# One staging buffer in place of two, and ten bias tiles in place of nine, in a fused attention and MLP kernel

## The chip, the cores and the metric
The kernel runs on one core of a Trainium2 chip. The time is that of one execution in device microseconds; a kernel is run several times and the median stands for it.

## The reference, cut to what matters
Attention with a position bias made by a small MLP, and then two MLPs, the output of each feeding the next, all in float32:

```
scores = (q @ k.T) / sqrt(64) + bias[h]          # 4 batches x 8 heads, 576 x 576
attn   = exp(scores - max) / sum                 # over the last axis
x      = (attn @ v) as 2304 tokens x 512
h = x @ w_in ;  x = (h * cos(h)) @ w_out         # 512 -> 2048 -> 512
h = x @ w_in2;  out = (max(h,0) + alpha*min(h,0)) @ w_out2
bias[h, i, j] = relu(log1p|i-j| / log1p(max(i,1)) * w1 + b1) @ w2
```

Weights are stored as float64. The kernel turns each into float32 on the chip and splits it into a high part (float32r) and a low part (the rest); a product is then three matrix products, high by high, high by low and low by high.

## The kernel before, in words
Tile, the framework, keeps a program order (the order in which the Python code makes the instructions), puts the instructions of each engine into an order of its own when all are known, and adds the waits. Engines and DMA queues execute in the order that it chose. A pool of tiles has a fixed number of buffers; a tile that finds none free waits for the last use of an older one.

The stages follow one another: the bias of all heads is written to DRAM (`bias_phase`); attention over 16 pairs (4 head pairs by 4 batches, the batch running fastest); `h_phase0` (first product of the first MLP, PE with one unit of 24 matmuls after another in three PSUM units); `o_phase(0)`; `h_phase1`; `o_phase(1)`. Attention runs 9 score blocks a pair; for each, PE makes the scores S (line 480), DVE adds the bias tile `bt` and takes the minimum (line 496), ACT takes the exponential (line 509); then PE transposes, ACT and DVE copy, and PE multiplies by v (lines 596 and 599). From pair 2's second unit on, lists fix the order of PE's work.

A pair of heads has nine bias tiles, one for each block, loaded on SP's queue by `load_bias` (line 417); they serve the four batches of a head pair. In the last batch, the loads of the next head pair's tiles are made block by block, each behind the last use of a tile. `BTB` (line 40) is the number of buffers: nine.

Beside attention, weights for `h_phase0` and `o_phase(0)` are prepared by generators that `step` advances a few pieces at a time, in program order:
- `wi` (line 302) does one of the 16 blocks of w_in: ACT, DVE and POOL turn it into float32 (`conv`), POOL makes the high part (line 316) and the low part (line 320). The first six stay in SBUF; the other ten go into a staging tile `st`, and an SP DMA writes them to `w_d` (line 323). `h_phase0` loads them again.
- `stage_wo` (line 273) does two blocks of w_out at a time: two `conv`, four sums of halves on DVE into the tile `ct` (line 280), then four groups in `leave_w` (line 259). For k from 3 to 7, five jobs, each group goes into a staging tile `sw`: ACT writes the high part (line 253), POOL the low part (line 255), and SP writes the tile to `w2_d` with one DMA (first group) or two (the other three), line 270. I call such a group a leaf.

`st` and `sw` share the tag `st`. During attention the tag lives in the pool `wst` with two buffers, which is closed at the end of attention (`sstack`). The pool `wt` has one buffer of the tag, used from `h_phase0` on, and one of `ct`.

Of the kernel before, what the change touches and what calls it, by code (L numbers as in the profile page):

```python
# [10 lines left out]
F32R = mybir.dt.float32r  # L11
# [25 lines left out]
HP, LP, XP, CPRI, SP = 200, 0, 300, -50, 400  # L37
HIA, LOP = 2, 1
UPB, EPB = {"D": 11, "A": 4}, 6
PBUF, BTB = 6, 9  # L40
FIRST, SIDE, SMOD, BFIRST, BRATE, SPL, WS0, WSR, PER = 4, 6, 2, 8, 2.5, 3, 28, 3.2, 1.0
SR = 2.0
NSP = 2
# [30 lines left out]
def attn_mlp_kernel(ctx: ExitStack, tc: tile.TileContext, a: dict, out: bass.AP):  # L74
# [95 lines left out]
    wpool = {}  # L170
# [7 lines left out]
    cstack = ExitStack()  # L178
    rstack = ExitStack()
    astack = ExitStack()  # L180
    sstack = ExitStack()
    raws_w = {}
    pinned = []
    anchor = []
# [32 lines left out]
    def conv(layer, f, part, box):  # L217
        nm = f"{layer}_{f}_{part}"
        if (layer, f, part) not in raws_w:
            load_raw(layer, f, part)  # L220
            yield
        raw = raws_w.pop((layer, f, part))
        signed = layer == 1 and part == 1
        if wide:
            c = wpool["c"].tile([128, 512], I32, tag="c", name=f"wc{nm}")
            p = wpool["c"].tile([128, 512], I32, tag="p", bufs=1, name=f"wp{nm}")
            hold(se.activation(out=c.bitcast(F32), in_=raw[:, :, 1].bitcast(F32), func=AF.Copy, scale=2.0 ** -112))
            hold(se.activation(out=p, in_=raw[:, :, 0].bitcast(U32), func=AF.Copy, scale=2.0 ** -29))
            yield
            if signed:  # L230
                ve.tensor_scalar(c, c, 3, zs[:, f:f + 1].bitcast(I32), op0=ALU.logical_shift_left, op1=ALU.bitwise_xor)
            else:
                hold(ve.tensor_scalar(c, c, 3, None, op0=ALU.logical_shift_left))
            hold(ve.scalar_tensor_tensor(out=c, in0=raw[:, :, 1], scalar=-2 ** 31, in1=c,  # L234
                                         op0=ALU.bitwise_and, op1=ALU.bitwise_xor))
            yield
            ge.tensor_tensor(out=c, in0=c, in1=p, op=ALU.add)  # L237
            yield
            box.append(c.bitcast(F32))
        else:  # L240
            if signed:
                ve.tensor_scalar(raw, raw, sgn[:, f:f + 1], None, op0=ALU.mult)
                yield
            box.append(raw)
# [7 lines left out]
    def split_to(hi, lo, w, eng=None):  # L252
        hold(se.activation(out=hi, in_=w, func=AF.Copy))
        yield
        hold((eng or (ve if pinned else ge)).tensor_tensor(out=lo, in0=w, in1=hi.bitcast(F32), op=ALU.subtract))
        yield
# [3 lines left out]
    def leave_w(layer, k, g, x):  # L260
        ps = GRPS[layer][g]
        n = len(ps)
        if (layer == 0 and k < NIP) or (layer == 1 and g < 3):
            w = WO[layer, g]
            yield from split_to(w[:, :, k, 0, :], w[:, :, k, 1, :], x)
            return
        st = wpool["t" if pinned else "st"].tile([128, 2, 2, 256], F32R, tag="st", name=f"sw{layer}_{k}_{g}")
        yield from split_to(st[:, 0:n, 0, :], st[:, 0:n, 1, :], x)
        for i, p in enumerate(ps):
            (ge if pinned else sy).dma_start(out=w2_d[layer][SLOT[p], :, k], in_=st[:, i].bitcast(F32))  # L270
        yield
# [3 lines left out]
    def stage_wo(layer, k):  # L275
        box = []
        yield from conv(layer, 2 * k, 1, box)
        yield from conv(layer, 2 * k + 1, 1, box)
        ct = wpool["t"].tile([128, 4, 256], F32, tag="ct", name=f"wt{layer}_{k}")
        sub = lambda o, u, v, op=ALU.subtract: hold(ve.tensor_tensor(out=o, in0=u, in1=v, op=op))  # L280
        c0, c1, c2, c3 = (ct[:, i] for i in range(4))
        u1, u2 = halves_of(box[0])
        v1, v2 = halves_of(box[1])
        if layer == 0:
            sub(c0, u2, v2, ALU.add)
            sub(c3, u1, u2)
            yield
            sub(c1, c0, u1)
            sub(c2, v1, c1)
            yield  # L290
            order = (cols(u1, 1), ct[:, 0:2], ct[:, 2:4], cols(box[1], 2))
        else:
            sub(c0, u2, u1)
            sub(c2, v2, u2)
            yield
            sub(c1, v2, c0)
            sub(c3, v1, c1)
            yield
            order = (cols(u1, 1), ct[:, 0:2], cols(box[1], 2), ct[:, 2:4])
        for g, x in enumerate(order):  # L300
            yield from leave_w(layer, k, g, x)

    def wi(layer, f):
        box = []
        yield from conv(layer, f, 0, box)
        if layer:
            t = wt[f] = wpool["h"][(f + 1) % 4].tile([128, 2, 512], F32R, tag="w", name=f"v{f}")
        elif f < NDIR:
            t = wt[f] = wpool["a"].tile([128, 2, 512], F32R, tag="w", name=f"w{f}")
        else:  # L310
            t = wpool["st"].tile([128, 2, 2, 256], F32R, tag="st", name=f"st{f}").rearrange("p a b c -> p a (b c)")
        hi, lo = t[:, 0], t[:, 1]
        if layer:
            se.activation(out=hi, in_=box[0], func=AF.Copy)
        elif HIA == 2:
            keep(0, ge.tensor_copy(out=hi, in_=box[0]))
        else:
            keep(0, se.activation(out=hi, in_=box[0], func=AF.Copy))
        yield
        keep(1, (ve if layer else ge).tensor_tensor(out=lo, in0=box[0], in1=hi.bitcast(F32), op=ALU.subtract))  # L320
        yield
        if not layer and f >= NDIR:
            sy.dma_start(out=w_d[f], in_=t.bitcast(F32))
            yield

    JOBS = [(wi, (0, f), 1.0, [(0, f, 0)]) for f in range(NF)]
    JOBS += [(stage_wo, (0, k), 3.0, [(0, 2 * k, 1), (0, 2 * k + 1, 1)]) for k in range(NIP, NK)]
    bg = []
# [24 lines left out]
    def attention():  # L353
        with ExitStack() as c:
# [63 lines left out]
            def load_bias(hp, s):  # L418
                t = bt_p.tile([128, S], F32, tag="bt", name=f"bt{hp}_{s}")
                if s == 0:  # L420
                    for i in range(2):
                        sy.dma_start(out=t[64 * i:64 * i + 64], in_=bias_rows(2 * hp + i, 512, S))
                else:
                    h, i = divmod(s - 1, 4)
                    rows = bias_rows(2 * hp + h, 128 * i, 128 * i + 128)
                    if h:
                        sy.dma_start(out=t[:, 64:S], in_=rows[:, 0:512])
                        sy.dma_start(out=t[:, 0:64], in_=rows[:, 512:S])
                    else:
                        sy.dma_start(out=t, in_=rows)  # L430
                bt[hp, s] = t
# [233 lines left out]
            def more_bias(g):  # L665
                nonlocal ng
                while ng < min(g, NG):
                    next(bias)
                    ng += 1
                    if ng >= SIDE and ng % SMOD == 0:  # L670
                        next(side, None)
                    for s, m in GNEED.items():
                        if ng == m:
                            for h in range(2 if s else 1):
                                load_bias(0, s + 4 * h)
                    if ng == NG:
                        for _ in side:
                            pass
                        bstack.close()
                        right = dict(side="right", reuse_waits="tile")  # L680
                        wpool["s"] = rstack.enter_context(tc.tile_pool(name="ws", bufs=2, **right))
                        wpool["c"] = rstack.enter_context(tc.tile_pool(name="wc", bufs=2, **right))
                        wpool["t"] = astack.enter_context(tc.tile_pool(name="wt", bufs=1, **right))
                        wpool["a"] = astack.enter_context(tc.tile_pool(name="wa", bufs=NDIR, **right))
                        wpool["x"] = astack.enter_context(tc.tile_pool(name="xh0", bufs=NCC, **right))
                        wpool["st"] = sstack.enter_context(tc.tile_pool(name="wst", bufs=2, **right))

            pend_exp = []
            fill = []
# [8 lines left out]
            while i < NS or pend_exp or waiting or fill:  # L698
                new = []
                if i < NS:  # L700
# [3 lines left out]
                    hp, b = pairs[n]  # L704
                    more_bias(max(BFIRST + int(BRATE * j), GNEED[s]))
                    for m in range(FIRST, NP):
                        f = pos[m, 1]
# [38 lines left out]
                else:  # L746
                    while fill and credit > 0:
                        d, fn, _ = fill.pop(0)
# [339 lines left out]
    def h_phase1():  # L1088
        runs = [[(0, 512), (512, 1024)], [(1024, 1536), (1536, 2048)], [(2048, 2304)]]
        with ExitStack() as c:  # L1090
# [38 lines left out]
            for k in range(NK):  # L1129
                for _ in range(2):  # L1130
                    if nw < NF:
                        bg.append(wi(1, nw))
                        nw += 1
                bg.append(stage_wo(1, k))
# [39 lines left out]
            step(1000)  # L1174

    attention()
    sstack.close()
    pinned.append(1)
    h_phase0()
    astack.close()  # L1180
# [70 lines left out]
```

## Time and profile before
| what | us |
|---|---|
| median of 3 runs | 1095.66 (1094.87 to 1096.27) |
| the profiled execution's own time | 1095.88 |
| its span in the trace | 1094.1 |
| PE busy | 1054.6 (96%) |
| DVE busy | 801.8 (73%) |
| ACT busy | 642.1 (59%) |
| POOL busy | 229.6 (21%) |

Shares are of the whole span. The slices of the page show PE at 8 tenths in those of 246 to 322 us, and at 9 tenths from there to the end. A stage is read best by its own stretch: the `wi` blocks are done until about 251 us, the five `stage_wo` jobs of attention between 248 and 328 us, attention's last product ends at 337 us.

### The profile page before, as it was taken

To read this page: it belongs to the slowest core of one execution; us is meant where nothing else is said; L and a number is where in the kernel's file an instruction comes from. 1 tells how busy PE (TensorE), PEld (TensorE's weight loads), DVE (VectorE), ACT (ScalarE), POOL (GpSimd) and SP (SyncE) were. 2 spreads that over 40 slices of the span, in tenths; PEclk is the share of its full clock that TensorE was granted. 3 is DMA by queue.
4 is the path that set the end of the run, shared out by engine and by line. 5 is a ranking of instruction groups with operands and counts; after the bars stand their busy time and mean duration, and the time that the engine had idled before them with its cause. 6 is when DMAs were issued, how large, how long until landed. Compare 5 with 4: busy or idle time off the path is not lost.

```text
span 1094.1 us, 18708 instructions
## 1 busy us (share of the span) xinstructions
PE 1054.6 (96%) x7024; PEld 891.2 (81%) x7024; DVE 801.8 (73%) x1292; ACT 642.1 (59%) x1076; POOL 229.6 (21%) x236
## 2 busy tenths in 40 slices
PE   6899999999889999999999999999999999999998
PEld 1346677777667889888899999988888889999998
DVE  7876778788875878778788777677756847777673
ACT  7995788788884555555454554466555534444442
POOL 0005676675550000010000000323222300000000
PEclk9899999999999999999999999999999999999999
DMA  9765748577659433436569171877655649554621
GB/s 331 213 174 159 229 140 293 199 237 253 220 182 390 163 136 128 146 135 229 205 208 306 46 254 66 334 253 224 221 202 185 222 165 358 161 201 130 217 72 46
DMA packets 107594, 219.76 MB, mean 201 GB/s; under 512 B 11504, under 2 KB 57328, under 8 KB 106096
## 3 DMA queue, kind: packets, MB, share of 16 engines
q1 hardware_dynamic: 77104, 157.74, 44.6%
q10 hardware_dynamic: 27968, 50.34, 12.2%
q0 software_dynamic: 2432, 10.49, 2.5%
q8 instruction: 55, 0.90, 0.3%
q14 instruction: 35, 0.29, 0.1%
HBM read 133.98 MB, written 84.56 MB: 200 GB/s over the span
## 4 chain that ended last, share of the span: by engine, by line
PE 78%; DVE 7%; DMA 6%; ACT 4%; issue 2%; POOL 1%; SPq 0%; ACTq 0%; DVEq 0%; POOLq 0%
PE v L1145 18%; PE h L811 16%; PE ob L1014 14%; PE oc L1014 9%; PE oa L1014 8%; PE S L480 5%; DVE P L496 2%; PE x_B L599 2%; PE T_A L574 1%; PE bps L142 1%; DVE wc L234 1%; ACT be L156 1%; PE T_B L574 1%; DMA w_d<-sw 1%; PE x_A L599 1%
## 5 line engine op out<-in xcount | busy, mean ns | idle before, releaser
L1145 PE MATMUL v<-x,v 128*128 128x512 f32 (+1 forms) x984 | 198.0, 364 | 0.0
L1145 PEld LDWEIGHTS v<-x,v 128*128 128x128 f32 x984 | 168.5, 189 | 29.5
L811 PE MATMUL h<-xhi,w 128*128 128x512 f32 (+1 forms) x640 | 183.9, 372 | 1.2 <-DMA w<-w_d 1.2
L237 POOL TENSOR_TENSOR wc<-wc,wp 128x512 int32<-128x512 int32 x64 | 86.5, 1351 | 285.6 <-DVE wc L234 232.7
L811 PEld LDWEIGHTS h<-xhi,w 128*128 128x128 f32 x640 | 116.0, 188 | 23.4 <-DVE tb L825 1.6
L996 ACT ACTIVATE op<-a 128x768 fp32r<-128x768 f32 x84 | 70.5, 844 | 84.6 <-PE ob L1014 27.3
L811 PE MATMUL h<-xlo,w 128*128 128x512 f32 (+1 forms) x320 | 118.7, 371 | 0.0
L997 DVE TENSOR_TENSOR op<-a,op 128x768 fp32r<-128x768 f32 x84 | 80.0, 956 | 51.7 <-ACT op L996 49.4
L496 DVE CUSTOM_DVE_ANT_0 P<-S,bt 128x576 f32<-128x576 f32 x128 | 91.8, 750 | 25.7 <-PE S L480 18.1
L509 ACT ACTIVATE P<-P,nm 128x576 f32<-128x576 f32 x128 | 99.1, 777 | 15.9 <-DVE nm L496 15.8
L996 ACT ACTIVATE op<-b 128x768 fp32r<-128x768 f32 x84 | 70.6, 844 | 62.5 <-PE ob L1014 22.2
L997 DVE TENSOR_TENSOR op<-b,op 128x768 fp32r<-128x768 f32 x84 | 79.7, 954 | 28.0 <-ACT op L996 27.7
L820 ACT ACTIVATE ta<-h,quart 128x1024 int32<-128x1024 f32 x36 | 40.1, 1114 | 67.7 <-PE h L811 48.5
L1156 DVE SCALAR_TENSOR_TENSOR u<-v,asg,u 128x1024 f32<-128x1024 f32 (+2 forms) x48 | 48.0, 1013 | 40.8 <-ACT u L1155 40.4
L1014 PE MATMUL ob<-op,wo 128*128 128x384 f32 x432 | 76.4, 336 | 0.0
L1014 PEld LDWEIGHTS ob<-op,wo 128*128 128x128 f32 x432 | 75.1, 188 | 0.0
L821 DVE SCALAR_TENSOR_TENSOR tb<-ta,h 128x1024 f32<-128x1024 int32 x36 | 43.8, 1218 | 35.1 <-ACT ta L820 33.5
L811 PEld LDWEIGHTS h<-xlo,w 128*128 128x128 f32 x320 | 60.4, 189 | 11.1
L1155 ACT ACTIVATE u<-v,sgn 128x1024 f32<-128x1024 f32 (+2 forms) x48 | 42.9, 897 | 41.7 <-PE v L1145 41.6
L234 DVE SCALAR_TENSOR_TENSOR wc<-raw,wc 128x512 int32<-128x512 int32 x64 | 59.8, 938 | 1.2
L824 ACT ACTIVATE tb<-tb,hpi 128x1024 f32<-128x1024 f32 x36 | 41.2, 1144 | 22.7 <-DVE tb L822 21.0
L1014 PE MATMUL oc<-wq,op 128*128 128x256 f32 x432 | 53.3, 283 | 0.2 <-DVE op L997 0.2
(154 smaller groups left out, 2077.9 us busy)
## 6 DMA issues: line engine op xcount, KB each, us to landing
a<-g_d SPq DMA_DIRECT2D x60, 384.0 KB, 4.5
g_d<-tb ACTq DMA_DIRECT2D x36, 512.0 KB, 2.9
b<-g_d SPq DMA_DIRECT2D x48, 384.0 KB, 4.9
raw<-in_wi_dram SPq DMA_DIRECT2D x32, 512.0 KB, 3.8
raw<-in_wo_dram SPq DMA_DIRECT2D x32, 512.0 KB, 4.2
g_d<-u ACTq DMA_DIRECT2D x28, 512.0 KB, 2.8
bias_d<-be SPq DMA_DIRECT2D x36, 295.5 KB, 3.4
w_d<-sw SPq DMA_DIRECT2D x35, 256.0 KB, 2.8
```

The source lines that it names most:

```text
L234: hold(ve.scalar_tensor_tensor(out=c, in0=raw[:, :, 1], scalar=-2 ** 31, in1=c, op0=ALU.bitwise_and, op1=ALU.bitwise_xor))
L237: ge.tensor_tensor(out=c, in0=c, in1=p, op=ALU.add)
L480: pe(te.matmul(ps[:, hf, 0:HS], lhsT=w[r, 128 * i:128 * i + 128], rhs=m[r, c0:c0 + HS], start=(j == 0), stop=(j == len(terms) - 1)))
L496: keep(2, ve.tensor_tensor_reduce(out=sn.rearrange("p (a b) -> p a b", a=2), in0=ps[:, :, 0:HS], in1=bt[hp, s].rearrange("p (a b) -> p a b ...
L509: exps.append(se.activation(out=e, in_=e, func=AF.Exp, bias=nm, scale=-1.0, accum_out=sums[n, u][:, col, 0:1]))
L811: te.matmul(ps[:, i], lhsT=w_[:, wx, w], rhs=xx[:, 0:n], start=(j == 0), stop=(j == 11))
L821: ve.scalar_tensor_tensor(out=g, in0=tt, scalar=-C1, in1=h, op0=ALU.mult, op1=ALU.add)
L996: se.activation(out=o[:, 0], in_=x, func=AF.Copy)
L997: lows.append(ve.tensor_tensor(out=o[:, 1], in0=x, in1=o[:, 0].bitcast(F32), op=ALU.subtract))
L1014: ins = te.matmul(ps[:, m], lhsT=x[:, sl] if L else w[:, sl], rhs=w if L else x, start=first, stop=kk == NK - 1 and n == 2, skip_group_che ...
L1145: ins = te.matmul(both[:, i, 0:a1 - a0], lhsT=w[:, wx, 128 * cc:128 * cc + 128], rhs=x[:, xx, cc, a0 - o:a1 - o], start=(n == 0), stop=(n ...
L1156: ve.scalar_tensor_tensor(out=g, in0=ps, scalar=asg[:, f:f + 1], in1=g, op0=ALU.mult, op1=ALU.max)
```

## The change
Ten bias tiles in place of nine. The pool `wst` with its two buffers goes; the staging tiles of attention, of `wi` and of `stage_wo`, are taken from the one buffer of the tag in the pool `wt`, which stays open to the end of `h_phase0`. Per partition that is 8192 bytes less and 2304 bytes more; tiles that lie behind the bias tiles move by 2304 bytes. What is computed is the same. The float32 scores of the first four pairs and the fixed lists from pair 2's second unit on, which the change's name also speaks of, are in both kernels.

```
-PBUF, BTB = 6, 9
+PBUF, BTB = 6, 10
...
-    sstack = ExitStack()
...
-        st = wpool["t" if pinned else "st"].tile([128, 2, 2, 256], F32R, tag="st", name=f"sw{layer}_{k}_{g}")
+        st = wpool["t"].tile([128, 2, 2, 256], F32R, tag="st", name=f"sw{layer}_{k}_{g}")
...
-            t = wpool["st"].tile([128, 2, 2, 256], F32R, tag="st", name=f"st{f}").rearrange("p a b c -> p a (b c)")
+            t = wpool["t"].tile([128, 2, 2, 256], F32R, tag="st", name=f"st{f}").rearrange("p a b c -> p a (b c)")
...
-                        wpool["st"] = sstack.enter_context(tc.tile_pool(name="wst", bufs=2, **right))
...
     attention()
-    sstack.close()
```

## Rows read from the trace of the kernel before

**Rows 1.** Windows: busy us and (instructions) of each engine, clock, DMA share, GB/s.
```profile
166.00:246.00 80.00, 77.25 (x705) 59.72 (x704) 64.02 (x158) 64.78 (x150) 56.73 (x58) 1.00 0.73 241
246.00:322.00 76.00, 65.58 (x588) 49.81 (x586) 64.20 (x151) 64.06 (x144) 42.09 (x40) 1.00 0.64 217
322.00:337.00 15.00, 14.79 (x101) 10.69 (x100) 4.51 (x11) 6.82 (x14) 3.02 (x3) 1.00 0.93 311
337.00:350.00 13.00, 11.79 (x52) 9.46 (x51) 9.37 (x10) 7.53 (x8) 1.28 (x1) 1.00 1.03 402
```
**Rows 2.** Timeline of DVE: the last instruction of a pair (start, duration).
```profile
148.95 0.49 DVE L615 TENSOR_TENSOR xe_B<-x_B,T_B 128x320 f32<-128x320 f32 x1
...
245.96 0.49 DVE L615 TENSOR_TENSOR xe_B<-x_B,T_B 128x320 f32<-128x320 f32 x1
...
282.58 0.49 DVE L615 TENSOR_TENSOR xe_B<-x_B,T_B 128x320 f32<-128x320 f32 x1
...
302.09 0.48 DVE L615 TENSOR_TENSOR xe_B<-x_B,T_B 128x320 f32<-128x320 f32 x1
...
321.93 0.47 DVE L615 TENSOR_TENSOR xe_B<-x_B,T_B 128x320 f32<-128x320 f32 x1
```
**Rows 3.** Chain of waits around attention's end (start, us, what).
```profile
339.06 10.06 DMA w<-w_d
349.26 111.79 PE h L811 x576
```
**Rows 4.** Timeline: leaves of three jobs on ACT, POOL and SP.
```profile
259.85 0.63 ACT L253 ACTIVATE sw<-wt 128x512 fp32r<-128x512 f32 x1 [0.27 <-DVE wt L280]
...
288.62 0.62 ACT L253 ACTIVATE sw<-wt 128x512 fp32r<-128x512 f32 x1
289.68 2.70 POOL L255 TENSOR_TENSOR sw<-wt,sw 128x512 fp32r<-128x512 f32 x2
289.69 0.61 ACT L253 ACTIVATE sw<-wt 128x512 fp32r<-128x512 f32 x1
290.97 0.80 SPq L270 DMA_DIRECT2D w_d<-sw  x2
...
299.16 0.42 ACT L253 ACTIVATE sw<-wc 128x256 fp32r<-128x256 f32 x1 [0.63 <-DMA w_d<-sw]
...
319.75 0.61 ACT L253 ACTIVATE sw<-wt 128x512 fp32r<-128x512 f32 x1
```
**Rows 5.** DMA issues: KB each, median us to landing; of 284 to 303 us.
```profile
w_d<-sw SPq DMA_DIRECT2D x8, 256.0 KB, 2.6
```
**Rows 6.** The same of 320 to 360 us, and of the whole span.
```profile
w_d<-sw SPq DMA_DIRECT2D x6, 256.0 KB, 5.7
...
w_d<-st SPq DMA_DIRECT2D x10, 512.0 KB, 4.6
```
**Rows 7.** ACT's instructions of `conv`, 262 to 322 us, by line.
```profile
L228 ACT ACTIVATE wp<-raw 128x512 int32<-128x512 uint32 x7 | 4.7, 673 | 4.1 <-POOL wc L237 4.1
L227 ACT ACTIVATE wc<-raw 128x512 f32<-128x512 f32 x7 | 4.7, 668 | 0.0
```
**Rows 8.** Waits of ACT, 245 to 330 us: total, times, longest.
```profile
ACT sw L253 <- DMA w_d<-sw: 2.1, 3, 0.9
```
**Rows 9.** Tile `sw`, 245 to 290 us: spread of the landings.
```profile
DMA to landing us min/median/max: 2.1/2.6/4.7
```
**Rows 10.** Waits of DVE, 262 to 322 us.
```profile
DVE wt L280 <- POOL wc L237: 2.5, 4, 1.1
```
**Rows 11.** Timeline of POOL and SP: two `wi` blocks.
```profile
212.32 1.28 POOL L320 TENSOR_TENSOR st<-wc,st 128x512 fp32r<-128x512 f32 x1
213.54 0.61 POOL L316 CAST st<-wc 128x512 fp32r<-128x512 f32 x1
214.60 0.38 SPq L323 DMA_DIRECT2D w_d<-st  x1
```
**Rows 12.** Waits of SP, 165 to 246 us, and of POOL, 240 to 262 us.
```profile
SPq L430 <- DVE nm L496: 3.6, 6, 0.8
...
POOL qh L458 <- DMA rq<-in_q_dram: 4.1, 1, 4.1
```
**Rows 13.** Waits of 322 to 360 us at PE.
```profile
PEld h L811 <- DVE tb L825: 1.6, 1, 1.6
PE h L811 <- DMA w<-w_d: 1.2, 1, 1.2
```

## The prediction
> **What bounds the kernel now.** I read the engines' busy time by stretch first, then the chain of waits, then the stretch that the change touches instruction by instruction. From 349 us on the chain of waits is PE, one matmul behind the other [rows 3]; nothing that the change does after attention lasts long enough to alter that. So the time is set by when PE gets through attention and through the change to the first MLP.
>
> Attention has two regimes. Beside the blocks of w_in, PE is busy 77.25 of 80 us [rows 1], and a pair takes (245.96 - 148.95)/6 = 16.17 us [rows 2]: PE is the bound. Beside the w_out jobs it is busy 65.58 of 76 us [rows 1], and a pair takes (321.93 - 245.96)/4 = 18.99 us [rows 2]. ACT and DVE are busy 64 of these 76 us each, about 84%, and in order; PE waits for them. PE idles 10.4 us there against 2.6 in as much time of the first regime: 7.8 us is the most that any relief can bring back. From 322 to 337 us PE is busy again (14.79 of 15), since units of the first MLP fill in, while ACT is busy for 6.8 and DVE for 4.5 us [rows 1]: there is room for displaced work.
>
> **The change part by part.** *A slower chain of leaves.* Now, with two buffers, a leaf's ACT instruction follows the one before it after 1.07 us (288.62, 289.69) [rows 4]. With one it waits until the DMAs of that leaf have landed: ACT at 288.62, POOL's low part until 291.0 (half of the 2.70), two DMA issues until 291.8, the second begun at 291.4, landing 2.6 us later [rows 5], so at 294.0. That is 5.4 us a leaf; the first leaf of a job, half as large with one DMA, I estimate at 4.4. A job thus takes at least 3 x 5.4 + 4.4 = 20.6 us, where the trace has (319.75 - 259.85)/4 = 14.98 [rows 4]. The last job's second leaf moves from 319.75 to about 259.85 + 4 x 20.6 = 342 us, behind attention.
>
> *Relief.* In 76 us there are 76/20.6 = 3.7 jobs in place of 5.1. A job is 2 x (0.668 + 0.673) + 3 x 0.62 + 0.42 = 4.96 us of ACT [rows 4, 7], so about 6.9 us of ACT leave the crowded stretch (and its share of DVE's and POOL's work) for the roomy one behind it. That lies between nothing and the 7.8 us above; since the load of a pair falls only by some 10%, I take half: -3.9.
>
> *New waits on ACT.* Behind a leaf's instruction on ACT stand the exponentials and the copies out of PSUM; DVE and PE wait for these. The order of ACT is fixed ahead, so a leaf costs what the landing is later than that order allows for. The trace shows this only where a third leaf came too soon for two buffers: three waits of 2.1 us in all, 0.7 each [rows 8]. Bounds: 0, where the order allows for the whole landing (other work then goes ahead), and 4.7 - 2.6 = 2.1 us, the longest landing over the median [rows 9]. Some 12 leaves fall into the crowded stretch: 12 x 0.7 = 8.4 us of waiting (0 to 25). ACT has 11.9 us idle there [rows 1], in which part of it disappears: the pair with the 0.63 us wait [rows 4] took 302.09 - 282.58 = 19.51 us and the next, without one, 19.84 [rows 2], so a wait isn't simply added. I take half, the value between none and all: +4.2 (0 to +12.6).
>
> The Trainium skill, in PSUM — Partial Sum Buffer, Engine vs sequencer instructions, says that the queues of ScalarE, VectorE and GpSimdE are strictly first in, first out. By that alone every microsecond of a leaf's wait would be paid by all behind it, 8.4 in place of 4.2 us; these two pairs don't bear it out as a price, since the engine had idle time anyway.
>
> *Tiles held longer.* `ct` and the converted blocks are read by the late leaves, so the next job's sums on DVE and conversions on ACT wait. Nearest are DVE's waits for the job's own data, 2.5 us in four [rows 10]: 0.6 for each of four jobs, half hidden as above: +1.2 (0 to +2.5).
>
> *The blocks of w_in.* Here POOL waits. The low part of a block ends at 213.60, its DMA is issued at 214.60 [rows 11] and lands 4.6 us later [rows 6], at 219.2; the next block's high part, now at 213.54, starts 5.7 us later. POOL has 23.3 us idle in 80 [rows 1], the next pair of blocks comes a pair later, and PE isn't waiting for POOL: 0. If that cover goes, a late split of q and k holds up S; I allow up to +2.
>
> *The tenth bias tile.* Nine tiles are in use until the last batch, so a load waits for the tile of its own block; six such waits on SP took 3.6 us over two head pairs' change [rows 12]. The tenth lets each load use the tile freed a block earlier. What is late next are the loads of q behind them in SP's queue, for which POOL waited 4.1 us once [rows 12], and a bias tile is needed only a pair later. At most -1; I take 0. The shift by 2304 bytes changes which attention tiles the first MLP's weights wait for; 0, within the bounds below.
>
> *The change to the first MLP.* Three leaves of the last job now fall at about 342, 347 and 353 us, where the DMA engines are full (share 1.03) [rows 1] and such a transfer lands after 5.7 us, 3.1 more [rows 6]. Each can hold ACT for that long in front of the first MLP's activations. PE waited there once already, 1.6 us for DVE [rows 13], so the three PSUM units cover only part of 3 x 3.1: I take +2 (0 to +5). The weights on which PE waited 1.2 us [rows 13] can come sooner, as fewer writes precede them, or later, if a load of w_out that needs the last job's first leaf stands in front of them in SP's queue: 0 (-1.2 to +3).
>
> Sum: -3.9 + 4.2 + 1.2 + 0 + 0 + 2 + 0 = +3.5 us on the profiled execution's own 1095.88, 1099.4. That execution is 0.2 above the median, so 1099.2 us.
>
> **The rivals.** *Relief wins.* The order allows for the landings, ACT hardly waits, and the work goes where there is room. For it: only 2.1 us of such waits in 20 leaves now [rows 8]. Against it: in all but a few of them the second buffer was there. -3.9 to -7.8, with +1 to +2 at the change of stage: about -4.5, 1091.
>
> *ACT and DVE pay every wait.* At 84% the engines have little slack of the right kind; each leaf's wait is passed on whole: -3.9 + 8.4 + 2.5 + 2 = +9, 1104.7. It decides from about 0.7 us a leaf on. Against it: the two pairs named above. The Trainium skill's rule of the strict queues would make it this one.
>
> *Nothing moves.* Most leaves' waits fall into idle time, and the relief is as small: ±1, 1095.7. For it: idle 11.9 us of ACT [rows 1]. It is also what would be seen if the tenth tile and the one buffer were both off the path.
>
> **How the numbers follow.** A measurement here can't tell less than 0.2%, 2.2 us, from no change. The forecast's case has 0.50, between about -1 and +7: 0.34 slower, 0.13 within, 0.03 faster. Relief 0.22: 0.19 faster, 0.03 within. Every wait paid 0.13, slower. Nothing moves 0.15: 0.13 within, 0.01 on each side. Together faster 0.23, same 0.29, slower 0.48. The range takes in the middle of the relief and all but the worst of the paid waits: 1090 to 1107; the likeliest case alone has 1095 to 1103.
>
> **What would show it.** Leaves some 5.4 us apart on ACT and jobs 20 us apart; the last leaves behind 340 us; ACT's waits for the DMAs of `sw` at 8 us or so in place of 2.1. Pairs of 18 to 20 us between 246 and 322 us: at 17 the relief has won, at 21 every wait is paid. PE's wait for the first MLP's weights near 1.2 us, and waits of ACT for `sw` behind 340 us with some idle time of PE behind them. Pairs at 16.2 us before 246 us, or the step on w_in's blocks is wrong. If the leaves are not much farther apart than now, the first step is wrong and all behind it.

## The result and the profile after

| kernel | median, us (runs) | ratio to before, 95% interval |
|---|---|---|
| before | 1095.41 (6) | 1 |
| after | 1104.74 (6) | 1.0083 [1.007, 1.0096] |

The change made the kernel 0.83% slower. The profiled execution of after is its slowest one, 1108.48 us, with a span of 1106.7 us; before's span was 1094.1.

Four stretches as in [rows 1], and one behind them (columns as there):
```profile
166.00:246.00 80.00, 75.28 (x680) 58.26 (x680) 61.63 (x150) 63.16 (x145) 52.25 (x53) 1.00 0.70 226
246.00:322.00 76.00, 66.81 (x556) 51.42 (x552) 50.82 (x129) 55.01 (x124) 29.95 (x31) 0.93 0.48 156
322.00:337.00 15.00, 14.51 (x116) 10.62 (x113) 9.71 (x26) 10.48 (x24) 5.42 (x6) 1.00 0.58 180
337.00:350.00 13.00, 11.83 (x73) 8.67 (x72) 4.63 (x8) 4.78 (x8) 3.29 (x3) 1.00 0.95 335
...
350.00:420.00 70.00, 66.54 (x286) 53.21 (x285) 56.12 (x61) 39.67 (x50) 15.53 (x13) 1.00 0.70 258
```
DVE and ACT are much less busy beside the leaves (50.82 and 55.01 us, 64 each before): work has left this stretch, though it also holds a little less of the pairs. But PE's mean clock falls to 0.93: 66.81 x 0.07 = 4.7 us of full speed lost. Beside w_in, PE is idle for 4.72 us instead of 2.75, and between 350 and 420 us for 3.46 instead of nothing (70.00 of 70.00 busy before).

Pair ends, as in [rows 2], and attention's last:
```profile
150.87 0.49 DVE L614 TENSOR_TENSOR xe_B<-x_B,T_B 128x320 f32<-128x320 f32 x1
...
249.80 0.49 DVE L614 TENSOR_TENSOR xe_B<-x_B,T_B 128x320 f32<-128x320 f32 x1
...
285.97 0.49 DVE L614 TENSOR_TENSOR xe_B<-x_B,T_B 128x320 f32<-128x320 f32 x1 [0.85 <-PE x_B L595]
308.50 0.48 DVE L614 TENSOR_TENSOR xe_B<-x_B,T_B 128x320 f32<-128x320 f32 x1
329.38 0.48 DVE L614 TENSOR_TENSOR xe_B<-x_B,T_B 128x320 f32<-128x320 f32 x1
346.52 0.49 DVE L614 TENSOR_TENSOR xe_B<-x_B,T_B 128x320 f32<-128x320 f32 x1 [3.79 <-PE x_B L595]
```
The pair between the third and the fourth of these took 22.5 us, where before's took 19.5. Attention ends 9.4 us later (337.16 before); what follows takes 760.2 us instead of 756.9.

Leaves on ACT, as in [rows 4] (the bracket is the idle time before the instruction and what ended it):
```profile
273.79 0.41 ACT L252 ACTIVATE sw<-wc 128x256 fp32r<-128x256 f32 x1
280.63 0.63 ACT L252 ACTIVATE sw<-wt 128x512 fp32r<-128x512 f32 x1 [1.97 <-DMA w_d<-sw]
286.97 0.62 ACT L252 ACTIVATE sw<-wt 128x512 fp32r<-128x512 f32 x1
293.80 0.63 ACT L252 ACTIVATE sw<-wc 128x512 fp32r<-128x512 f32 x1 [3.53 <-DMA w_d<-sw]
300.71 0.41 ACT L252 ACTIVATE sw<-wc 128x256 fp32r<-128x256 f32 x1
...
398.06 0.63 ACT L252 ACTIVATE sw<-wt 128x512 fp32r<-128x512 f32 x1 [1.31 <-DVE wt L279]
```
Here they stand 6.3 to 6.9 us apart and a job takes 26.9 (273.79 to 300.71; the next one takes 24.3). Eight of the twenty start behind attention, the last of them at 412.75 us, 66 behind. PE at the fourth of them:
```profile
294.96 1.22 PE L595 MATMUL x_A<-T_A,v 128*128 128x256 f32 x2 [2.85 <-ACT T_A L558]
```
The copy T_A stands right behind the leaf in ACT's order (294.33), so the leaf's wait of 3.53 us became 2.85 us of idle PE. The windows behind it:
```profile
293.00:296.00 3.00, 1.04 (x3) 0.86 (x4) 0.00 (x0) 2.21 (x5) 1.27 (x1) 0.72 0.02 7
296.00:299.00 3.00, 3.00 (x15) 2.98 (x14) 1.19 (x3) 1.97 (x5) 0.00 (x0) 0.50 0.60 219
299.00:302.00 3.00, 3.00 (x22) 2.38 (x22) 2.03 (x4) 1.77 (x5) 0.74 (x1) 0.64 0.00 0
```
The granted clock is 0.50, the lower of its two levels (1.2 GHz), right after that idle time. It happens again between 317 and 323 us (0.71 and 0.72 in two windows of 3 us).

Waits of 245 to 330 us (as [rows 8]), and waits at PE of 340 to 420 us (as [rows 13]):
```profile
ACT sw L252 <- DMA w_d<-sw: 8.4, 4, 3.5
...
PE h L809 <- DVE tb L823: 2.7, 2, 2.3
```
PE's wait for the first MLP's weights is 0.7 us, 1.2 before. The last block of w_in is now written at 269.96 us, 18.6 later than before (251.34):
```profile
269.96 0.32 SPq L322 DMA_DIRECT2D w_d<-st  x1
```

### The profile page after: what moved, and what is told of

Read it like the earlier page. It is cut to its first block, busy times and chain, and to the rows that moved or that the text cites. A ratio compares the mean times of both kernels' runs of the same rounds, so it can differ in the third digit from the quotient of the medians.

```text
span 1106.7 us, 18702 instructions
## 1 busy us (share of the span) xinstructions
PE 1058.9 (96%) x7024; PEld 894.9 (81%) x7024; DVE 800.7 (72%) x1292; ACT 644.0 (58%) x1076; POOL 230.1 (21%) x236
## 4 chain that ended last, share of the span: by engine, by line
PE 72%; DVE 9%; DMA 8%; ACT 5%; issue 3%; POOL 1%; SPq 1%; ACTq 0%; POOLq 0%; DVEq 0%
PE v L1143 18%; PE ob L1012 14%; PE oc L1012 9%; PE oa L1012 8%; PE h L809 8%; PE S L479 5%; DMA w_d<-sw 3%; PE x_B L598 2%; PE T_B L573 2%; DMA w<-w_d 2%; PE bps L142 2%; DVE P L495 2%; PE T_A L573 1%; DVE tb L819 1%; DVE wc L233 1%
## 5 line engine op out<-in xcount | busy, mean ns | idle before, releaser
L233 DVE SCALAR_TENSOR_TENSOR wc<-raw,wc 128x512 int32<-128x512 int32 x64 | 54.8, 859 | 1.4
L1012 PE MATMUL ob<-wp,op 128*128 128x256 f32 x432 | 52.8, 282 | 0.0
```

The source lines that it names most:

```text
L1012: ins = te.matmul(ps[:, m], lhsT=x[:, sl] if L else w[:, sl], rhs=w if L else x, start=first, stop=kk == NK - 1 and n == 2, skip_group_che ...
```

## The experiments

By ratio to before, times 1095.4 us:

| kernel | tiles, leaf's high part on | ratio, interval | us against before |
|---|---|---|---|
| e1 one buffer | nine, ACT | 0.9985 [0.9974, 0.9996] | -1.6 |
| after | ten, ACT | 1.0083 [1.007, 1.0096] | +9.1 |
| e8 one buffer | nine, POOL | 0.9939 [0.9925, 0.9954] | -6.7 |
| e4 one buffer | ten, POOL | 0.9962 [0.9948, 0.9976] | -4.2 |
| e6 one buffer | ten, order of nine, ACT | 0.9993 [0.9984, 1.0003] | -0.8 |
| e10 one buffer, later jobs | nine, ACT | 1.0072 [1.005, 1.0095] | +7.9 |
| e9 one buffer, later jobs | ten, ACT | 1.0057 [1.0037, 1.0077] | +6.2 |

**One staging buffer alone.** The kernel after with nine tiles:
```
-PBUF, BTB = 6, 10
+PBUF, BTB = 6, 9
```


> One staging buffer, nine bias tiles. Theory A (the single staging buffer costs the time; the tenth tile is off the path): 1104 us, within 2 of the changed kernel's 1104.7. Rival B (the tenth tile and the shift of the tiles behind it cost it): 1096 to 1098. Rival C (the tenth tile gains a little that the staging buffer's loss covers): 1107 or more.

Measured: 1094.89 us, 0.9985, so theory A falls. The staging buffer costs nothing here, though the leaves are late as well and ACT waits for their landings 16.3 us in eleven instructions (245 to 420 us; 2.1 before). Its stretches from 246 us on, three pair ends, and the first leaves of two jobs:
```profile
246.00:322.00 76.00, 68.70 (x615) 52.27 (x614) 58.96 (x146) 60.23 (x137) 34.46 (x35) 1.00 0.53 182
322.00:337.00 15.00, 14.15 (x83) 10.54 (x82) 7.15 (x15) 8.10 (x17) 5.44 (x6) 1.00 0.79 272
337.00:350.00 13.00, 11.54 (x51) 9.18 (x51) 9.29 (x8) 7.36 (x8) 3.20 (x2) 1.00 1.03 401
350.00:420.00 70.00, 68.79 (x298) 55.44 (x297) 60.56 (x68) 39.69 (x51) 14.95 (x11) 1.00 0.64 230
```
```profile
245.91 0.49 DVE L614 TENSOR_TENSOR xe_B<-x_B,T_B 128x320 f32<-128x320 f32 x1
...
316.86 0.47 DVE L614 TENSOR_TENSOR xe_B<-x_B,T_B 128x320 f32<-128x320 f32 x1
336.30 0.48 DVE L614 TENSOR_TENSOR xe_B<-x_B,T_B 128x320 f32<-128x320 f32 x1
```
```profile
310.51 0.42 ACT L252 ACTIVATE sw<-wc 128x256 fp32r<-128x256 f32 x1
...
332.46 0.42 ACT L252 ACTIVATE sw<-wc 128x256 fp32r<-128x256 f32 x1 [1.43 <-DMA w_d<-sw]
```
The clock stays at 1.00. Four pairs take 70.95 us where before's took 75.97 [rows 2]: 5.0 us gained. The last pair takes 19.4 us where before's took 15.2, but 2.1 of these 4.2 us are matmuls of the first MLP done earlier (8.87 us of them in that pair, 6.81 before). PE's idle time says it more directly: against before it is 3.1 us less from 246 to 322 us, and from 322 to 420 us it is 2.1 more (3.52 against 1.42). The Trainium skill, in Trainium Kernel Development and Optimization, Best Practices, advises double-buffering for performance; here, at this pace of the jobs, one buffer in place of two was, if anything, 0.15% faster.

**One buffer for one of the two stages.** Both kernels keep before's two buffers; a dummy tile holds one, either from the first block of w_in to the first leaf (e2, cut here to where the tile is taken) or from there to the last leaf (e3):
```
...
+            wpool["hold"] = wpool["st"].tile([128, 2, 2, 256], F32R, tag="st", name="taken")
+            ge.memset(wpool["hold"].bitcast(F32)[:, 0, 0, 0:1], 0.0)
...
```


> Nine bias tiles, two staging buffers, one of which a dummy tile holds until the first leaf of w_out: one buffer for the blocks of w_in, two for the leaves. If the loss comes from the leaves (theory A1): 1096 to 1098, and the blocks of w_in end at about 270 us in place of 251 with pairs still near 16.5 us. If it comes from POOL's waits and the late start of the leaves (theory A2): 1100 to 1105. Both halves: about 1100, as the late start pushes leaves behind attention.

> Nine bias tiles, two staging buffers for the blocks of w_in, and one for the leaves of w_out, the other held by a dummy tile from the first leaf to the last. Theory A1 (the leaves cost it): 1101 to 1104, ACT's waits for the DMAs of the leaves 8 us or more inside attention. Theory A2 (the blocks of w_in cost it): 1096 to 1097.

Measured: 1118.8 us, 1.0205 [1.0188, 1.0221], and 1124.38, 1.0252 [1.0231, 1.0273]. Both are far slower than after and outside every range that I had named. Waits of e2, 330 to 420 us:
```profile
PE h L815 <- DVE tb L829: 20.5, 1, 20.5
...
ACT sw L253 <- DMA w_d<-sw: 13.6, 2, 11.3
```
PE stands still for 20 us at the change to the first MLP (27.7 in e3), and the clock falls to 0.80 to 0.85 over 350 to 420 us. In this layout, with the pool of two buffers open to attention's end, late leaves meet the start of the first MLP; in e1, with late leaves too but one buffer, PE has no such stop. The stop hides what the runs were to tell apart, so they don't say which of the two stages pays.

**The leaf's high part on POOL.** In `split_to`, for the leaves of attention:
```
...
-        hold(se.activation(out=hi, in_=w, func=AF.Copy))
+        if on_pool:
+            hold(ge.tensor_copy(out=hi, in_=w))
+        else:
+            hold(se.activation(out=hi, in_=w, func=AF.Copy))
...
-        yield from split_to(st[:, 0:n, 0, :], st[:, 0:n, 1, :], x)
+        yield from split_to(st[:, 0:n, 0, :], st[:, 0:n, 1, :], x, on_pool=not pinned)
```
e4 is the kernel after with this, e8 is e1 with it, e7 is the kernel before with it, and e2p is e2 with it.

> The changed kernel, with the high part of a leaf written by POOL instead of ACT during attention: the chain of leaves is as long or longer (1.3 us in place of 0.6 on the first step at most), but ACT no longer waits for a landing. If ACT's waits in order are the price (theory A1): 1097 to 1100, pairs of 16.5 to 18 us between 250 and 330 us. If the late leaves behind attention or PE's lower clock of their own are the price: 1103 to 1107.

> One staging buffer, nine bias tiles, and the high part of a leaf on POOL instead of ACT. ACT waited 16 us for leaves in the same kernel with ACT. If such waits are paid even where the sum came out even (theory P: relief hides them): 1087 to 1091, better than the kernel before. If they fell into idle time: 1093 to 1095.

> The kernel before (two buffers, nine tiles), with the high part of a leaf on POOL. ACT waits only 2.1 us for leaves there, and 2.3 us of ACT's work a job move to POOL. Theory P: 1090 to 1094, a gain by the load taken from ACT only. If one buffer was itself a gain (by spreading the jobs): slower than the same with one buffer and nine tiles.

> The kernel with one buffer for w_in's blocks, two for the leaves and a dummy tile (1118.8 us), with the high part of a leaf on POOL. Its trace has one leaf that waits 11.3 us on ACT at the change to the first MLP, and PE idle for 20.5 us behind it. If ACT's wait in order is the cause: 1092 to 1098. If the late loads of weights or of x are: 1112 or more.

Measured: e4 1092.93 us, 0.9962; e8 1089.15, 0.9939; e7 1109.71, 1.0127 [1.011, 1.0144]; e2p 1115.54, 1.0175 [1.0158, 1.0192]. e8 lies in the range of the theory that such waits are paid; e4 lies 4 us below its range, and e7 16 us above its own. e8 is the fastest version of all and beats both kernels. Its stretches and its waits of 245 to 340 us:
```profile
246.00:322.00 76.00, 70.75 (x627) 54.74 (x627) 59.59 (x150) 57.97 (x132) 37.55 (x43) 1.00 0.51 168
322.00:337.00 15.00, 15.00 (x87) 11.31 (x87) 6.98 (x9) 6.54 (x9) 4.97 (x5) 1.00 1.00 363
337.00:350.00 13.00, 13.00 (x58) 10.58 (x57) 8.53 (x8) 5.59 (x6) 2.01 (x3) 1.00 1.03 398
```
```profile
POOL sw L253 <- DMA w_d<-sw: 25.5, 8, 4.8
```
The waits are longer than on ACT, 25.5 us, but no wait of PE for POOL shows from 245 to 340 us, and PE is never idle from 322 to 420 us. Moving the leaf's high part off ACT is worth 5 us with nine tiles (0.9985 to 0.9939) and 13 with ten (1.0083 to 0.9962).

That is the worth of the whole move, not of the waits alone: ACT also has 0.6 us less to do for each leaf, and the order changes with it. e7 makes the same move where ACT waited for landings only 2.1 us [rows 8]:
```profile
246.00:322.00 76.00, 69.00 (x619) 52.77 (x618) 60.76 (x152) 57.38 (x129) 41.16 (x49) 1.00 0.56 191
```
PE is busy 3.4 us longer there than before (65.58), where e8 gains 2.05 over e1. So in this stretch the work taken off ACT can make most or all of e8's gain, and the 5 us can't be read as the price of e1's waits.

With the leaves on POOL, the tenth tile costs only some 2.5 us (e4 against e8, whose intervals overlap a little), where with the leaves on ACT it costs 10.7 (after against e1). About three quarters of its price thus need leaves on ACT. What is left fits the stretch beside w_in, where e4's PE is idle as long as after's (e8 has 77.26 busy there):
```profile
166.00:246.00 80.00, 75.28 (x682) 58.15 (x683) 61.28 (x150) 63.13 (x144) 51.78 (x53) 1.00 0.69 227
```
In e7 and e2p, with two buffers, PE again stands still at the change to the first MLP. Since e2p has no leaf of these jobs on ACT, a leaf's wait there isn't what stops PE in e2; its expectation's other case, late loads, came true. Waits of e7, of 330 to 420 us, and its SP queue's over the same time:
```profile
PE h L814 <- DVE tb L828: 18.1, 1, 18.1
ACT xhi L795 <- DMA xlo<-x_d: 16.8, 1, 16.8
```
```profile
SPq L191 <- DMA g_d<-tb: 55.8, 6, 18.3
```
On SP the loads of `xlo` wait for the stores of a tile `tb`, ACT waits for them, and PE for ACT and DVE.

**Ten tiles in the order of nine.** Each load of the next head pair's bias is made to wait for its own block's DVE instruction, as it does where nine tiles are all in use:
```
-                            load_bias(hp + 1, s + 4 * h)
+                            load_bias(hp + 1, s + 4 * h, maxes[s + 4 * h])
```


> The changed kernel with ten bias tiles, but every load of the next head pair's bias made to wait for the DVE instruction of its own block, as with nine. Every engine then has the same instructions in the same order as with nine tiles and one buffer (1094.9 us); only addresses differ. Theory P (the tenth tile costs time because it lets loads go earlier, which re-orders the engines so that leaves fall on worse places): 1094 to 1096. Rival S (the shift of the later tiles by 2304 bytes changes who waits for whose memory): 1101 to 1105.

Measured: 1095.37 us, 0.9993, as theory P had it. Every engine's order is now that of e1; only the addresses of tiles are those of after. So neither the memory nor the shift by 2304 bytes costs anything: what costs is the order that the free tile permits, together with the earlier loads that come with it (this run sets back both). The conversion's place in it shows in DVE's timeline, first of after, then of e1, about the same score block:
```profile
182.43 0.49 DVE L614 TENSOR_TENSOR xe_B<-x_B,T_B 128x320 f32<-128x320 f32 x1
182.87 0.69 DVE L560 COPY T_A<-T_A 128x512 f32<-128x512 f32 x1
184.13 0.43 DVE L232 TENSOR_SCALAR wc<-wc 128x512 int32<-128x512 int32 x1 [0.57 <-ACT wc L226]
184.59 1.09 DVE L233 SCALAR_TENSOR_TENSOR wc<-raw,wc 128x512 int32<-128x512 int32 x1
185.60 0.75 DVE L495 CUSTOM_DVE_ANT_0 P<-S,bt 128x576 f32<-128x576 f32 x1
```
```profile
181.44 0.49 DVE L614 TENSOR_TENSOR xe_B<-x_B,T_B 128x320 f32<-128x320 f32 x1
181.87 0.69 DVE L560 COPY T_A<-T_A 128x512 f32<-128x512 f32 x1
182.48 0.42 DVE L232 TENSOR_SCALAR wc<-wc 128x512 int32<-128x512 int32 x1
182.93 0.69 DVE L233 SCALAR_TENSOR_TENSOR wc<-raw,wc 128x512 int32<-128x512 int32 x1
183.54 0.75 DVE L495 CUSTOM_DVE_ANT_0 P<-S,bt 128x576 f32<-128x576 f32 x1
```
From the pair's end to P it is 3.17 us in after and 2.10 in e1. In after, ACT did the exponential and only then this conversion's first step (183.43); DVE waited for it with P behind. PE then waited 1.05 us for `nm` before S at 187.18. Over 166 to 246 us these waits add up, after and then e1:
```profile
PE S L479 <- DVE nm L495: 4.6, 4, 1.8
```
```profile
PE S L479 <- DVE nm L495: 1.5, 2, 0.8
```

**Half of the loads held.** In e11 only those of the last change of head pairs wait as in e6 (`if hp == 2`), in e12 only those of the first two (`if hp < 2`). In e11 the engines' order is practically after's; in e12 it is e1's up to the last change and after's from there.

> Ten tiles, one staging buffer; the bias loads of the last change of head pairs alone go behind their own block's DVE operation, as with nine tiles, the two changes before are as in the kernel after. Theory (the price of the tenth tile is the order that the earlier changes bring about): all of it is still there, 1103 to 1106 us, and the clock falls again near 293 to 302 us. Rival (the loads of the last change, which stand beside the w_out leaves, make the loss): 1095 to 1098 us.

> The other half: the loads of the first two changes of head pairs are held as with nine tiles, those of the last change are as in the kernel after, and with them the engines' order from there on. Theory (some 4 us are lost beside the blocks of w_in, some 6 beside the leaves, where the order is that of the kernel after): 1099 to 1102 us, pairs up to 246 us as with nine tiles. Rival (all of the loss follows from the shift that the first part makes): 1095 to 1097 us. Second rival (all of it lies beside the leaves): 1103 to 1106 us.

Measured: e11 1103.44 us, 1.0056 [1.0039, 1.0073]; e12 1102.32, 1.0051 [1.0031, 1.0071]. Both are slow: 7.8 and 7.2 us over e1 by ratio, where after is 10.7 over it. The parts don't add up, so my split into 4 and 6 us is not borne out. e11 fell into its interval; e12 lies between its own (to 1102) and that of a loss wholly beside the leaves (from 1103), and doesn't decide between them. Up to 246 us e12's pairs are as with nine tiles (245.70 us; 245.91 in e1, 249.80 in after), so its whole loss lies behind that. The rival that the last loads make the whole loss falls with e11, the one that the first ones do with e12. The clock fell in each, but not where I had said for e11: at 284 to 290 us (0.77 and 0.66). In e12:
```profile
308.00:311.00 3.00, 2.13 (x10) 1.83 (x9) 2.10 (x7) 2.61 (x6) 0.96 (x2) 0.72 0.46 169
311.00:314.00 3.00, 3.00 (x24) 2.73 (x22) 1.33 (x3) 2.72 (x7) 1.85 (x2) 0.71 0.18 62
```

**Another place for the leaves.** `WS0` sets where in the program order the w_out jobs start; nothing else is touched. e9 is after with it, e10 is e1 with it:
```
-FIRST, SIDE, SMOD, BFIRST, BRATE, SPL, WS0, WSR, PER = 4, 6, 2, 8, 2.5, 3, 28, 3.2, 1.0
+FIRST, SIDE, SMOD, BFIRST, BRATE, SPL, WS0, WSR, PER = 4, 6, 2, 8, 2.5, 3, 31, 3.2, 1.0
```


> The kernel after with the start of the w_out jobs in the program order moved by WS0 = 31 in place of 28, nothing else. Theory (a leaf's wait costs by what stands behind it at its place, so that where the leaves fall decides): moves by several us, 1095 to 1102, and no fall of the clock near 295 us. Rival (ten tiles cost 9 to 10 us over nine whatever the place of the leaves): 1103 to 1107.

> Nine tiles and one staging buffer with the same WS0 = 31. Theory (the place of the leaves decides): 1092 to 1101 us, and the difference between ten and nine tiles at this pace is another than 9.8 us, between 3 and 7. Rival (fixed price of the tenth tile): 9 to 10 us below the kernel with ten tiles and this pace, 1093 to 1097.

Measured: e9 1102.7 us, 1.0057; e10 1103.05, 1.0072. Nine tiles with one buffer, level with before at 28, are 8 us slower at 31, above my interval. The kernel before wasn't run at 31, so whether that is the one buffer's or the pace's is open. The tenth tile, 10.7 us at 28, costs nothing that can be told at 31 (I had said 3 to 7), and e9 itself lies between its two intervals. A fixed price of the tenth tile falls; that the place decides is borne out in kind, not in size. The clock didn't fall near 295 us in e9, as I had said, but it did at 225 to 228 us (0.53). A window of e10:
```profile
314.00:317.00 3.00, 3.00 (x15) 2.81 (x14) 1.42 (x4) 2.90 (x7) 2.52 (x2) 0.50 0.13 44
```
In windows of 3 us from 100 to 340 us, the clock is below 0.95 somewhere in each of the five slow kernels with one buffer (after, e9 to e12) and nowhere in before, e1, e4, e6 and e8. In e9 to e12 I estimate what the falls cost at some 1.6 us each (PE's busy time in these windows, times what the clock lacks), so most of their 6 to 8 us is something else.

Not tried: ten tiles with two buffers, two buffers at the pace of 31, and three buffers.

## Why the prediction came out

The sign was right and the number near (1099.2 forecast, 1104.74 measured, inside 1090 to 1107), but the reason was wrong, so that the range held is luck. My sum of +3.5 was made of the one staging buffer's costs; that buffer alone measures -1.6 (e1). The loss came with the tenth tile, which I had put at nothing. The rival by which ACT and DVE pay every wait had 1104.7, the measured time almost to the tenth; that is luck too, since e1 has the waits and not the loss.

- **The tenth tile: the step that failed.** "At most -1; I take 0": 10.7 us instead. I asked only which load could start sooner, and took the order of everything else as given (the waits that I read there are also those of one line; two other lines of the same loads waited 2.1 us more). But the framework orders all instructions anew when a load becomes free earlier. DVE's and ACT's conversions went in front of P beside w_in, which remains with the leaves on POOL (2.5 us); the rest needs leaves on ACT, whose waits fell on worse places, as at 293.80 us.
- **Slower chain of leaves: right for one buffer.** 20.6 us a job forecast, 21.95 in e1's rows. In after it is 26.9 and 24.3. Two of the four gaps in the job shown are longer by ACT's order; in the other two the transfer landed about 4.5 us after its issue (last issues at 276.09 and about 289.4 us, next leaves at 280.63 and 293.80), where I had taken 2.6.
- **Relief, new waits, tiles held longer: priced wrong in sum.** -3.9, +4.2 and +1.2 make +1.5 us beside the leaves; e1's PE idle time there falls by 3.1, from 10.42 to 7.30. The three aren't measured apart. The waits themselves were right in length (8.4 us forecast; over 245 to 330 us 9.7 in e1, 8.4 in after), so either their price was too high or the relief larger. The rival by which each is paid whole would make e1's 16.3 us cost 16; the move to POOL, which takes them off ACT, is worth 5 with ACT's lighter load included. The Trainium skill's strict queues (PSUM — Partial Sum Buffer, Engine vs sequencer instructions) agree with the row of `T_A`, which starts right behind the late leaf at 294.33 us, but the rule taken as a price does not come out. In after, PE stood idle for most of one wait (2.85 of 3.53) and then ran at the lower clock.
- **Blocks of w_in, 0: right for what I argued.** They end 12.2 us later in e1 (263.52), and its PE is as busy as before's in 166 to 246 us, 77.25 us. With ten tiles it isn't (75.28), and pairs there take 16.5 us, where I had named 16.2 as the sign of being right: the miss comes with the tenth tile's order.
- **The change to the first MLP, +2: right in size for one buffer.** PE idles 2.1 us more than before from 322 to 420 us in e1 and 3.7 more in after. But not three leaves fall behind attention, the last at 353 us: it is seven in e1 and eight in after, the last at 391.68 and 412.75.

In profiled executions, after's span is 13.7 us above e1's. Of these, 4.7 us is the slower clock in 246 to 322 us; 2.0, 1.9 and 2.3 us are more idle time of PE in 166 to 246, 246 to 322 and 350 to 420 us; 1.3 is there at the first pair (103.65 against 102.34, but e8 has 103.54 too); in 322 to 350 us after idles 0.7 less. That is 11.5; the rest lies outside these stretches.

Open: which of the changed places makes the part of the loss that needs leaves on ACT, as e11 and e12 don't add up; how much of a leaf's price is its wait and how much the work on ACT; why e10 loses as much with nine tiles; and what the clock falls on: before had PE idle for 2.53 us at 281.74 without a fall, e12 2.49 at 289.39, e9 2.93 at 291.93.

## What to carry to other kernels

Where a planner orders the instructions, a resource set free can be a new order for every engine: compare the orders before putting a price on the resource, and test it by holding the new freedom back (e6), which separates memory from order. The length of a wait is not its price: e8 waits longer than e1 and is 5 us faster. Its waits stand on an engine for which PE doesn't wait, and ACT has less to do; the runs don't separate the two. A price can also hang on another choice: the tenth tile costs 10.7 us with the leaves on ACT and 2.5 with them on POOL. And a pace that is a plain number (`WS0` here) holds for one order: three steps of it cost nine tiles 9.5 us (e1 to e10), as much as the whole change, so a change is tried at several paces before it is judged.

## What the runs showed of the hardware

PE's granted clock can halve inside a stage that is busy on the whole: 0.50 in 296 to 299 us of after, behind 2.85 us of idle time, at a cost of up to 4.7 us in 76, with no such fall in the kernels that lost nothing. At the hand-over between stages, with the DMA engines full, ACT waited 11.3 us for one staging tile (e2, DMA share 1.01 from 337 to 349 us): the four transfers of such tiles issued in that time landed after 9.5 us in the median, against 2.6 in [rows 5].
